# Attention and two MoE layers on one core: half of the mixed chunk's scores issued later, single scaling of maxima, and a higher rate of quad sums

## Chip, core and metric

The kernel runs on one core of one Trainium2 chip. The metric is the device time of one execution in microseconds (us). The engines are named as in the profile: PE (TensorE matmul) and PEld (its weight loads), DVE (VectorE), ACT (ScalarE), POOL (GpSimd), and SP (SyncE), which here only issues DMAs.

## What is computed

```python
# q, k, v: (4 batches, 12 heads, 448, 64); float32
q_n, k_n = rmsnorm(q, g_q), rmsnorm(k, g_k)
scores = q_n @ k_n.T / 8
scores = scores - max(scores, -1)
attn = exp(scores); attn = attn / sum(attn, -1)
x = (attn @ v)                         # to (1792, 768)
x = relu(x @ w_in) ** 2 @ w_out        # d_ff 2048
a, b = x @ w1, x @ w2                  # 768 -> 1024
out = ((a * b) @ w3) @ w_out2          # 1024 -> 1024 -> 768
```

## The kernel before

Every product is made from a high and a low part of each operand (three matmuls for one of float32), so PE has 5958 matmuls, most of 448 columns. The weights come in units of 128 rows; each is loaded by SP, split by ACT (high part) and by DVE or POOL (low part, line 150) into a tile named `hl`, and used by PE at lines 411 to 413.

A loop goes over 48 heads, `h` from 0 to 47, twelve to a batch; the text calls heads 0 to 11 batch one, 12 to 23 batch two and so on. Beside the attention of head `h`, `fill(n)` issues about `n` matmuls of the MoE of an earlier batch from a generator (`gen_moe`); what a call of `fill` issues beyond its number is taken off the next. So PE always has MoE matmuls between the attention's steps, and PE works in the order in which it is given its instructions.

The scores of a pair of heads (an even one and the odd one after it) are made in seven chunks of 128 queries: 0 to 3 for the even head, 4 to 6 for the odd one. Chunk 3 is mixed: 64 of its rows are the last queries of the even head, the other 64 belong to the odd head, so its first two matmuls read the odd head's transposed keys `kt`. These are made by `stage_k(h + 1)`: PE transposes (line 941), ACT copies the bank to SBUF (`kt<-kv`, line 144). From batch two on, `stage_k(h + 1)` stands one `fill` ahead of `stage_qk(h, 1)`, which makes chunks 2 and 3.

Each chunk's scores go to one of two PSUM banks (`ps_sc`). DVE takes the row maximum out of the bank (line 967, into a column of `nb`), ACT computes the exponentials from the bank (line 991, `p<-sc,nb,rr`), and only then may the bank be written again. In batch one (`h < H`) DVE also multiplies the maxima by `rq` (line 969), once for the two chunks of a stage; later ACT does that for each chunk (line 988). From batch two on the exponentials are written to SBUF as `p`, copied by a DMA to `pw` (line 1015), transposed by PE in four pieces `stage_t(h - 1, 0)` to `(h - 1, 3)` (line 1045) into two banks `pt`, and each of these is copied by ACT and has its low part subtracted by DVE (`ptr<-pt,ptr`, line 150, in `stage_lo`); then its bank is free.

For the last two batches the second MoE is computed by a scheme with sums of quarters ("quads") of its weights. `gen_sums` makes them: four loads (`quad<-f`, `quad<-w3o`), four subtractions on the engine that `drip` names, four stores (`qs<-quad`). `use`, called once for each weight unit that PE uses, calls `drip_one`, which lets `rate` such steps go. During the last `gen_moe` the engine is DVE. There, after each product `x @ w_in`, `relu2` has ACT take the relu `r` out of PSUM and square it, DVE make `gf` (line 487), and POOL make the low part of `act` (line 150) that PE needs in the product with `w_out`.

The order on each engine is set by a scheduler that goes by priorities and readiness; SP keeps the written order from batch three on, and all engines do in the last stretch.

Of the kernel before, what the change touches and what calls it, by code (L numbers as in the profile page):

```python
# [8 lines left out]
F32 = mybir.dt.float32  # L9
# [6 lines left out]
ALU = mybir.AluOpType  # L16
# [14 lines left out]
def attention_moe_kernel(  # L31
# [15 lines left out]
    nc = tc.nc  # L47
    SP, ACT, DVE, POOL, PE = (e.engine for e in (nc.sync, nc.scalar, nc.vector, nc.gpsimd, nc.tensor))
    B, P, H, C, D = k_nat.shape
# [6 lines left out]
    NFC = w_in.shape[0] // 2  # L56
    KX = w_in.shape[2] // 64
    NE = w_out.shape[0] // 4
# [36 lines left out]
    small = ctx.enter_context(tc.tile_pool(name="small", bufs=4))  # L95
# [170 lines left out]
    drip = {"eng": "g", "rate": 0.0, "due": 0.0}  # L266
# [294 lines left out]
    def later(steps, fn, *args):  # L561
        tasks.append((tail["now"] + steps, len(tasks), fn, args))
# [78 lines left out]
    def gen_pair():  # L641
# [36 lines left out]
        for e in range(NQ):  # L678
            later(2 + 4 * e, form3, 1, e)
            later(14 + 4 * e, form3, 2, e)  # L680
        drip.update(eng="v", rate=5 * 12 / (2 * NFC + 2 * NE))
        for y in gen_moe(B - 1, added):
            if tail["on"]:
                tick()
# [65 lines left out]
        n = NIC // 2  # L750
        todo4 = [(k, i) for k in ORDER4[1:] for i in range(n)]
        d = [{} for _ in range(NQ)]
# [38 lines left out]
    def load_group(g):  # L791
        if not (0 <= g < NH // GH):
            return
        b, h0 = divmod(g * GH, H)
        qk = t1.tile([128, GH * C, D], F32, name="qn", tag="qn")
        qn = qk[:, :GH // 2 * QC]
        kn = t2.tile([P, GH, C, D], F32, name="kn", tag="kn")
        if g == 0:
            nc.sync.dma_start(out=kn[:, 0:2], in_=k_nat[0, :, 0:2])
            load_head(0)  # L800
            nc.sync.dma_start(out=qn[:, :QC], in_=q_nat[0, :, 0])
            load_to(0)
            nc.sync.dma_start(out=kn[:, 2:], in_=k_nat[0, :, 2:GH])
            nc.sync.dma_start(out=qn[:, QC:], in_=q_nat[0, :, 1])
            load_to(1)
        else:
            nc.sync.dma_start(out=kn, in_=k_nat[b, :, h0:h0 + GH])
            nc.sync.dma_start(
                out=qn, in_=q_nat[b, :, h0 // 2:(h0 + GH) // 2].rearrange("p j c d -> p (j c) d")
            )  # L810
        grp[g] = [qk, kn, None, None]

    def load_head(h):
        if not (0 <= h < NH):
            return
        b, hh = divmod(h, H)
        t = t2.tile([128, S], F32, name="qt", tag="qt")
        nc.sync.dma_start(out=t, in_=q_t[b, hh])
        qts[h] = t

    def load_v(h):
        if not (0 <= h < NH):
            return
        b, hh = divmod(h, H)
        t = t2.tile([128, C, D], F32, name="v", tag="v")
        nc.sync.dma_start(out=t, in_=v_in[b, hh])
        vs[h] = t
# [115 lines left out]
        copy_on("a", kt, ps[:, :S].bitcast(F32))  # L943
        d["kt"] = kt

    def stage_qk(h, s):
        if not (0 <= h < NH):
            return
        d = heads[h]
        nb = d["nb"] = small.tile([128, 2], F32, name="nb", tag="nb")  # L950
        chunks = CHUNKS[h % 2][s]
        n = len(chunks)
        o = d["sc"] = [None] * n

        def score(out, d, at, m):
            nc.tensor.matmul(out, d["qh"][:, at:at + m], d["kt"], start=True, stop=False)  # L956
            nc.tensor.matmul(out, d["ql"][:, at:at + m], d["kt"], start=False, stop=True)  # L957

        for j, c in enumerate(chunks):
            ps = ps_sc.tile([128, 512], F32, name="sc", tag="sc")  # L960
            o[j] = ps[:, :S]
            if c == 3:
                score(o[j], heads[h + 1], S - 128, 128)
                score(o[j][:MIX], d, S - MIX, MIX)
            else:
                score(o[j], d, (c % 4) * 128, 128)
            nc.vector.tensor_reduce(out=nb[:, j:j + 1], in_=o[j], axis=AX.X, op=ALU.max, negate=True)  # L967
        if h < H:
            nc.vector.tensor_tensor(  # L969
                out=nb[:, :n], in0=nb[:, :n], in1=d["rq"][:, chunks[0]:chunks[0] + n], op=ALU.mult  # L970
            )

    def stage_exp(h, s):
        if not (0 <= h < NH):
# [143 lines left out]
    def fill(n):  # L1118
        state["credit"] += n
        while state["gen"] is not None and state["credit"] > 0:  # L1120
            try:
                k = next(state["gen"])
                state["credit"] -= k
                state["left"] -= k
            except StopIteration:
                state["gen"] = None
# [4 lines left out]
    def gen_late():  # L1131
# [15 lines left out]
        out=gg, in0=g_sb[:, 0:1], scalar=float(D) ** -0.5, in1=g_sb[:, 1:2], op0=ALU.mult, op1=ALU.mult  # L1147
# [8 lines left out]
    for h in range(NH + 1):  # L1156
        n = W3O / ((H + 1) * 6) if h <= H else (MOE / (H * 6) if h <= 2 * H else (MOE + IN) / (2 * H * 6))
        late = h > 2 * H
        if h < 2:
            load_head(h + 3)  # L1160
            load_v(h + 1)
        if not late and h % GH == 0:
            load_group(h // GH + 1)
        stage_qk(h, 0)
        fill(n)
        if h <= 2 * H + 1:
            stage_sums(h - 1)
        stage_exp(h, 0)
        if h > 2 * H:
            stage_words(h, 0)  # L1170
        if h == 0:
            group_prep(0, "rest")
        if h >= 2:
            load_head(h + 3)
            load_v(h + 1)
        if late and h % GH == GH - 1:
            load_group((h + 1) // GH + 1)
        if h % H != 1:
            stage_x(h - 2)
        stage_t(h - 1, 0)  # L1180
        stage_t(h - 1, 1)
        early = H <= h and h % 2 == 0
        fill(n)
        if early:
            stage_k(h + 1)
        stage_lo(h - 1)
        if h < NH:
            v_prep(h)
        fill(n)
        if h <= 2 * H:  # L1190
            stage_words(h, 0)
        stage_rows(h - 1)
        even = H <= h
        if even:
            stage_qk(h, 1)
        if not early:
            stage_k(h + 1)
        stage_t(h - 1, 2)
        stage_t(h - 1, 3)
        fill(n)  # L1200
        stage_lo(h - 1)
        if not even:
            stage_qk(h, 1)
            fill(n)
        stage_exp(h, 1)
        if h > 2 * H:
            stage_words(h, 1)
        fill(n)
        if even:
            fill(n)  # L1210
        if h <= 2 * H:
            stage_words(h, 1)
        stage_v(h - 1)
        if h >= 2 * H and h % GH < 2:
            group_prep(h // GH + 1, "qk"[h % GH])
        elif h % GH == 1:
            group_prep(h // GH + 1)
        head_prep(h + 2)
        if h and h % H == 0:
            if h != 3 * H:  # L1220
                fill(1e9)
            stage_x(h - 1)
            if h == H:
                start_fill(gen_moe(0), MOE)
            elif h == 2 * H:
                in_order(SP)
                start_fill(gen_late(), MOE + IN)
            elif h == NH:
                start_fill(gen_pair(), MOE)
# [61 lines left out]
```

## Time and profile before

| | |
|---|---|
| median of three runs | 1153.86 us (1152.88 to 1155.03) |
| the profiled execution's own time | 1159.42 us |
| its span, first to last instruction | 1157.6 us |
| mean granted clock of TensorE | 0.99 |
| busy: PE, DVE, ACT, POOL | 97%, 68%, 67%, 53% of the span |

The profiled execution took 0.48% longer than the median; durations and waits below are its own. Busy shares are means over stages of different kinds; PE's matmuls are pipelined, so that a busy PE can still be at half clock. The stretch of batch one is about 14 to 170 us, of batch two 170 to 416, of batches three and four 416 to 860; after that come the last MoE parts.

### The profile page before, as it was taken

The page shows a single profiled execution, that of the slowest core. Times are in us where ns is not written, and L with a number is a line of the kernel's source. Part 1 is how long each engine was busy: PE and PEld are TensorE (multiplying, and loading weights), DVE is VectorE, ACT ScalarE, POOL GpSimd, SP SyncE. Part 2 cuts the span into 40 slices and gives each one's busy share as a digit, 9 for nine tenths or more (in the row PEclk, how much of TensorE's full clock was granted, in tenths as well). Part 3 has the DMA queues.
Part 4 walks back from the last instruction along what each step waited for, and adds up shares of the span by engine and source line. Part 5 has one row for each costly group of instructions (what it writes and reads, how often), then busy time and mean ns, then how long its engine had stood idle before and what let it go on. Part 6 is the DMA issues. An engine that isn't in the chain of part 4 may idle for free.

```text
span 1157.6 us, 18785 instructions
## 1 busy us (share of the span) xinstructions
PE 1124.8 (97%) x5958; PEld 1019.5 (88%) x5958; DVE 790.3 (68%) x1363; ACT 776.6 (67%) x1768; POOL 608.9 (53%) x609
## 2 busy tenths in 40 slices
PE   7789999999999999999999999999999999999998
PEld 4678888999889899989989899999999899999997
DVE  6889888878898854565674755564544315887886
ACT  6889978888878866767776666776764435533352
POOL 3375433445545455957876776684865854011131
PEclk8899999999999999999999999999999999999999
DMA  7867757898998863565655657665556664243423
GB/s 237 264 201 211 235 160 243 306 297 293 321 294 276 279 190 120 165 213 178 219 172 163 207 182 236 197 197 165 171 170 202 215 193 126 69 135 105 130 83 123
DMA packets 130899, 229.74 MB, mean 198 GB/s; under 512 B 17472, under 2 KB 84544, under 8 KB 130800
## 3 DMA queue, kind: packets, MB, share of 16 engines
q1 hardware_dynamic: 129072, 225.79, 61.3%
q10 hardware_dynamic: 1728, 2.75, 0.7%
q8 instruction: 47, 0.77, 0.3%
q14 instruction: 52, 0.43, 0.1%
HBM read 162.53 MB, written 37.05 MB: 172 GB/s over the span
## 4 chain that ended last, share of the span: by engine, by line
PE 67%; ACT 12%; DMA 7%; DVE 7%; issue 3%; POOL 1%; SPq 1%; DVEq 0%; ACTq 0%; POOLq 0%
PE mm L411 16%; PE mm L412 16%; PE mm L413 16%; PE kv L1091 4%; PE pt L1045 3%; PE sc L956 2%; ACT p L991 2%; PE sc L957 2%; ACT raw L333 2%; ACT hl L144 2%; DMA raw<-wo 1%; DVE raw L346 1%; ACT ptr L144 1%; DMA raw<-w_in 1%; DMA raw<-w_out 1%
## 5 line engine op out<-in xcount | busy, mean ns | idle before, releaser
L150 POOL TENSOR_TENSOR hl<-raw,hl 128x384 fp32r<-128x384 f32 (+1 forms) x286 | 333.1, 1171 | 289.6 <-ACT hl L144 245.7
L144 ACT ACTIVATE hl<-raw 128x384 fp32r<-128x384 f32 (+1 forms) x405 | 227.8, 566 | 152.5 <-PE mm L413 40.1
L411 PE MATMUL mm<-x,hl 128*128 128x448 f32 (+1 forms) x640 | 238.3, 372 | 1.2 <-ACT x L144 1.2
L412 PE MATMUL mm<-x,hl 128*128 128x448 f32 (+1 forms) x640 | 234.2, 366 | 0.8 <-DVE x L150 0.8
L413 PE MATMUL mm<-x,hl 128*128 128x448 f32 (+1 forms) x640 | 233.7, 365 | 0.2 <-DVE hl L150 0.2
L411 PE MATMUL mm<-act,hl 128*128 128x448 f32 (+1 forms) x544 | 201.6, 371 | 1.9 <-ACT act L144 1.9
L412 PE MATMUL mm<-act,hl 128*128 128x448 f32 (+1 forms) x544 | 198.8, 365 | 3.7 <-DVE act L150 2.0
L413 PE MATMUL mm<-act,hl 128*128 128x448 f32 (+1 forms) x544 | 197.9, 364 | 0.1
L967 DVE TENSOR_REDUCE nb<-sc 128x1 f32<-128x448 f32 x168 | 102.6, 615 | 73.8 <-PE sc L957 72.4
L411 PEld LDWEIGHTS mm<-x,hl 128*128 128x128 f32 x640 | 121.0, 189 | 10.9 <-ACT x L144 2.3
L412 PEld LDWEIGHTS mm<-x,hl 128*128 128x128 f32 x640 | 121.0, 189 | 10.4 <-DVE x L150 1.8
L413 PEld LDWEIGHTS mm<-x,hl 128*128 128x128 f32 x640 | 120.9, 189 | 9.8 <-DVE hl L150 0.5
L991 ACT ACTIVATE p<-sc,nb,rr 128x448 f32<-128x448 f32 x168 | 121.3, 723 | 11.5 <-DVE nb L969 8.8
L150 DVE TENSOR_TENSOR ptr<-pt,ptr 128x512 fp32r<-128x512 f32 (+1 forms) x144 | 85.9, 617 | 57.9 <-ACT ptr L144 57.4
L412 PEld LDWEIGHTS mm<-act,hl 128*128 128x128 f32 x544 | 102.8, 189 | 12.3 <-DVE act L150 3.0
L411 PEld LDWEIGHTS mm<-act,hl 128*128 128x128 f32 x544 | 102.8, 189 | 9.5 <-ACT act L144 2.3
L413 PEld LDWEIGHTS mm<-act,hl 128*128 128x128 f32 x544 | 102.8, 189 | 8.0 <-DVE hl L150 0.4
L339 POOL TENSOR_SCALAR raw<-raw 128x384 uint32<-128x384 uint16 (+1 forms) x80 | 57.2, 716 | 83.1 <-DMA raw<-w_out 20.7
L346 DVE SCALAR_TENSOR_TENSOR raw<-raw 128x384 uint32<-128x384 uint32 (+1 forms) x120 | 86.4, 728 | 18.5 <-POOL raw L339 9.6
L956 PE MATMUL sc<-kt,qh 128*128 128x448 f32 (+1 forms) x192 | 74.8, 389 | 14.3 <-ACT p L991 7.4
L150 DVE TENSOR_TENSOR hl<-raw,hl 128x384 fp32r<-128x384 f32 (+1 forms) x119 | 80.0, 675 | 7.9 <-ACT hl L144 7.8
L333 ACT ACTIVATE raw<-raw 128x384 f32<-128x384 f32 (+1 forms) x120 | 71.6, 601 | 15.6 <-DMA raw<-w_in 7.7
(153 smaller groups left out, 2122.0 us busy)
## 6 DMA issues: line engine op xcount, KB each, us to landing
pw<-p SPq DMA_DIRECT2D x54, 448.0 KB
raw<-f_in SPq DMA_DIRECT2D x96, 192.0 KB
raw<-f_out SPq DMA_DIRECT2D x72, 256.0 KB
raw<-w_in SPq DMA_DIRECT2D x32, 384.0 KB
raw<-w_out SPq DMA_DIRECT2D x24, 512.0 KB
raw<-w SPq DMA_DIRECT2D x32, 384.0 KB
qt<-q_t SPq DMA_DIRECT2D x48, 224.0 KB
raw<-f SPq DMA_DIRECT2D x56, 192.0 KB
```

Of the source, the lines that this page charges most:

```text
L144: return nc.scalar.activation(out=out, in_=in_, func=AF.Copy)
L150: return (nc.vector if eng == "v" else nc.gpsimd).tensor_tensor(out=out, in0=in0, in1=in1, op=op)
L333: nc.scalar.activation(out=hi, in_=hi, func=AF.Prelu, scale=2.0**-112, alpha=-(2.0**32))
L339: nc.gpsimd.tensor_scalar(out=t[:, :n, 0], in0=low, scalar1=2.0**-13, scalar2=2.0**-14 - 0.5, op0=ALU.mult, op1=ALU.add)
L346: nc.vector.scalar_tensor_tensor(out=f[:, :n].bitcast(U32), in0=t[:, :n, 1], scalar=3, in1=t[:, :n, 0], op0=ALU.logical_shift_left, op1=AL ...
L411: nc.tensor.matmul(ps, w[:, 0, wk, :], x[0], start=(i == 0), stop=False)
L412: nc.tensor.matmul(ps, w[:, 0, wk, :], x[1], start=False, stop=False)
L413: nc.tensor.matmul(ps, w[:, 1, wk, :], x[0], start=False, stop=(i == last))
L956: nc.tensor.matmul(out, d["qh"][:, at:at + m], d["kt"], start=True, stop=False)
L967: nc.vector.tensor_reduce(out=nb[:, j:j + 1], in_=o[j], axis=AX.X, op=ALU.max, negate=True)
L991: nc.scalar.activation(out=p, in_=o[j], func=AF.Exp, scale=d["rq"][:, c:c + 1], bias=nb[:, j:j + 1], accum_out=sm[:, c:c + 1],)
L1091: nc.tensor.matmul(ps[:, :S], w, m, start=(n == 0), stop=(n == len(ops) - 1))
```

## The change

From batch two on, the stage's second chunk (the mixed one, of an even head) is no longer issued next to the first: the transposes `stage_t(h - 1, 2)` and `(h - 1, 3)` and half of the following `fill(n)` stand between them. In batch one each chunk's maximum is multiplied by itself, right behind its reduction, in place of one multiplication for the stage. The rate of the steps of the quad sums in the last `gen_moe` goes from 60/44 to 60/40 for each weight unit (`NFC` is 16, `NE` is 6).

```diff
-        drip.update(eng="v", rate=5 * 12 / (2 * NFC + 2 * NE))
+        drip.update(eng="v", rate=5 * 12 / (2 * NFC + 2 * NE - 4))
...
-    def stage_qk(h, s):
+    def stage_qk(h, s, part=None):
...
-        nb = d["nb"] = small.tile([128, 2], F32, name="nb", tag="nb")
         chunks = CHUNKS[h % 2][s]
-        n = len(chunks)
-        o = d["sc"] = [None] * n
+        if part != 1:
+            d["nb"] = small.tile([128, 2], F32, name="nb", tag="nb")
+            d["sc"] = [None] * len(chunks)
+        nb, o = d["nb"], d["sc"]
...
         for j, c in enumerate(chunks):
+            if part not in (None, j):
+                continue
...
             nc.vector.tensor_reduce(out=nb[:, j:j + 1], in_=o[j], axis=AX.X, op=ALU.max, negate=True)
-        if h < H:
-            nc.vector.tensor_tensor(
-                out=nb[:, :n], in0=nb[:, :n], in1=d["rq"][:, chunks[0]:chunks[0] + n], op=ALU.mult
-            )
+            if h < H:
+                nc.vector.tensor_tensor(
+                    out=nb[:, j:j + 1], in0=nb[:, j:j + 1], in1=d["rq"][:, c:c + 1], op=ALU.mult
+                )
...
         if even:
-            stage_qk(h, 1)
+            stage_qk(h, 1, 0)
         if not early:
             stage_k(h + 1)
         stage_t(h - 1, 2)
         stage_t(h - 1, 3)
-        fill(n)
+        if early:
+            fill(n / 2)
+            stage_qk(h, 1, 1)
+            fill(n / 2)
+        else:
+            fill(n)
```

Three places of the order show what this moves. The first is PE in head 18 (batch two): `sc` are score matmuls (the pair with 64 rows ends the mixed chunk), `pt` the transposes, `mm` the MoE. Before:

```order
L413 MATMUL mm<-x,hl 128x448
L956 MATMUL sc<-kt,qh 128x448
L957 MATMUL sc<-kt,ql 128x448
L956 MATMUL sc<-kt,qh 128x448
L957 MATMUL sc<-kt,ql 128x448
L956 MATMUL sc<-kt,qh 64x448
L957 MATMUL sc<-kt,ql 64x448
L1045 MATMUL pt<-ident_r,pw 128x128 x3
L1045 MATMUL pt<-ident_r,pw 64x128 x3
L411 MATMUL mm<-x,hl 128x448
```

The same place on PE in the changed kernel, whose lines have moved by one and by three:

```order
L413 MATMUL mm<-x,hl 128x448
L957 MATMUL sc<-kt,qh 128x448
L958 MATMUL sc<-kt,ql 128x448
L1048 MATMUL pt<-ident_r,pw 128x128 x3
L1048 MATMUL pt<-ident_r,pw 64x128 x3
L411 MATMUL mm<-x,hl 128x448
L412 MATMUL mm<-x,hl 128x448
L413 MATMUL mm<-x,hl 128x448
...
L957 MATMUL sc<-kt,qh 128x448
L958 MATMUL sc<-kt,ql 128x448
L957 MATMUL sc<-kt,qh 64x448
L958 MATMUL sc<-kt,ql 64x448
```

The mixed chunk's four matmuls now stand behind six transposes and six MoE matmuls (three of them left out above). So it is at the other even heads from 14 on, with nine MoE matmuls at 16 and 24; at head 12 the place is nearly as before.

The second place is DVE in batch one, at the second stage of head 6: two reductions of chunks 2 and 3 and the scaling of their maxima, `nb<-nb,rr`. Before:

```order
L967 TENSOR_REDUCE nb<-sc 128x1
L150 TENSOR_TENSOR ptr<-pt,ptr 128x384
L150 TENSOR_TENSOR pte<-pt,pte 64x384
L967 TENSOR_REDUCE nb<-sc 128x1
L863 TENSOR_REDUCE ss_107<-qn 112x16
L969 TENSOR_TENSOR nb<-nb,rr 128x2
L925 SCALAR_TENSOR_TENSOR ql<-qt,gg,qh 128x448
```

The same place on DVE in the changed kernel:

```order
L150 TENSOR_TENSOR pte<-pt,pte 64x384
L970 TENSOR_REDUCE nb<-sc 128x1 x2
L972 TENSOR_TENSOR nb<-nb,rr 128x1
L925 SCALAR_TENSOR_TENSOR ql<-qt,gg,qh 128x448
L972 TENSOR_TENSOR nb<-nb,rr 128x1
L346 SCALAR_TENSOR_TENSOR raw<-raw_1447 128x384
L863 TENSOR_REDUCE ss_107<-qn 128x14
```

The first maximum is scaled directly behind the two reductions, and a long reduction of another stage (line 863) no longer stands ahead of it. In all of batch one 42 such scalings stand where 24 stood, and many neighbours on every engine have changed places.

The third place is DVE in the last `gen_moe`, where PE makes `x @ w_in` for the first half (eight `gf`, here the first eight of the list), with the subtractions of three quads. Before:

```order
L487 TENSOR_TENSOR gf<-mm,r 128x448 x2
L150 TENSOR_TENSOR quad<-quad 128x512 x2
L487 TENSOR_TENSOR gf<-mm,r 128x448
L150 TENSOR_TENSOR quad<-quad 128x512 x2
L487 TENSOR_TENSOR gf<-mm,r 128x448 x3
L150 TENSOR_TENSOR quad<-quad 128x512
L487 TENSOR_TENSOR gf<-mm,r 128x448
L150 TENSOR_TENSOR quad<-quad 128x512 x3
L487 TENSOR_TENSOR gf<-mm,r 128x448
```

The same place on DVE in the changed kernel:

```order
L487 TENSOR_TENSOR gf<-mm,r 128x448 x2
L150 TENSOR_TENSOR quad<-quad 128x512 x4
L487 TENSOR_TENSOR gf<-mm,r 128x448 x4
L150 TENSOR_TENSOR quad<-quad 128x512 x3
L487 TENSOR_TENSOR gf<-mm,r 128x448
L150 TENSOR_TENSOR quad<-quad 128x512
L487 TENSOR_TENSOR gf<-mm,r 128x448
```

Ahead of the eighth `gf`, the last of the half, one subtraction stands where three stood, and three stand ahead of the seventh where one stood; on SP the loads of these quads stand up to one weight load earlier.

## Rows read from the trace of the kernel before

**Rows 1.** Page, parts 1 and 2: busy time; granted clock by fortieths of the span.

```profile
PE 1124.8 (97%) x5958; PEld 1019.5 (88%) x5958; DVE 790.3 (68%) x1363; ACT 776.6 (67%) x1768; POOL 608.9 (53%) x609
...
PEclk8899999999999999999999999999999999999999
```

**Rows 2.** PE's waits in the whole program: total us, times, longest.

```profile
PE sc L956 <- ACT p L991: 7.4, 8, 2.1
PE sc L956 <- ACT kt L144: 6.8, 7, 1.8
```

**Rows 3.** The same view from 165 to 420 us and from 420 to 870.

```profile
PE sc L956 <- ACT kt L144: 3.6, 3, 1.8
...
PE sc L956 <- ACT kt L144: 3.0, 3, 1.5
```

**Rows 4.** Timeline of PE, heads 18, 20, 22, 28, 32, 36: start, us, idle before.

```profile
292.79 0.36 PE L956 MATMUL sc<-kt,qh 128*128 128x448 f32 x1
292.99 0.37 PE L957 MATMUL sc<-kt,ql 128*128 128x448 f32 x1
294.87 0.47 PE L956 MATMUL sc<-kt,qh 128*128 128x448 f32 x1 [1.51 <-ACT kt L144]
...
295.79 0.38 PE L1045 MATMUL pt<-ident_r,pw 128*128 128x128 f32 x3
...
339.81 0.47 PE L956 MATMUL sc<-kt,qh 128*128 128x448 f32 x1 [0.35 <-ACT kt L144]
...
382.88 0.47 PE L956 MATMUL sc<-kt,qh 128*128 128x448 f32 x1 [1.75 <-ACT kt L144]
...
513.07 0.47 PE L956 MATMUL sc<-kt,qh 128*128 128x448 f32 x1 [1.48 <-ACT kt L144]
...
586.53 0.47 PE L956 MATMUL sc<-kt,qh 128*128 128x448 f32 x1 [0.92 <-ACT kt L144]
...
659.34 0.47 PE L956 MATMUL sc<-kt,qh 128*128 128x448 f32 x1 [0.58 <-ACT kt L144]
```

**Rows 5.** Timeline of DVE: low parts of the transposes, heads 18, 22, 28.

```profile
293.24 1.00 DVE L150 TENSOR_TENSOR ptr<-pt,ptr 128x384 fp32r<-128x384 f32 x2
...
380.36 1.02 DVE L150 TENSOR_TENSOR ptr<-pt,ptr 128x384 fp32r<-128x384 f32 x2 [0.37 <-ACT ptr L144]
...
511.28 1.02 DVE L150 TENSOR_TENSOR ptr<-pt,ptr 128x384 fp32r<-128x384 f32 x2 [2.09 <-ACT ptr L144]
```

**Rows 6.** Stretches behind two waits: busy us by engine, granted clock (PEclk), DMA.

```profile
384.40:387.70 3.30, 3.30 (x10) 2.91 (x10) 3.30 (x7) 2.63 (x7) 1.82 (x2) 0.50 0.85 299
...
513.10:516.50 3.40, 3.40 (x21) 3.04 (x22) 2.92 (x5) 3.22 (x10) 2.79 (x3) 1.00 0.85 225
```

**Rows 7.** Head 14: the mixed chunk's exponential on ACT, the next score in its bank.

```profile
216.16 0.76 ACT L991 ACTIVATE p<-sc,nb,rr 128x448 f32<-128x448 f32 x1
...
219.78 0.36 PE L956 MATMUL sc<-kt,qh 128*128 128x448 f32 x1
```

**Rows 8.** Batch one on DVE: a stretch, the scaling's group, its durations, one of them.

```profile
30.00:120.00 90.00, 78.77 (x412) 67.42 (x411) 82.73 (x150) 78.11 (x174) 49.77 (x56) 0.92 0.76 230
...
L969 DVE TENSOR_TENSOR nb<-nb,rr 128x2 f32<-128x2 f32 (+1 forms) x24 | 8.5, 354 | 0.1
...
L969 DVE TENSOR_TENSOR nb<-nb,rr x24: 143/158/1123, 18.8 to 169.5; 128x2 f32<-128x2 f32 x18, 128x1 f32<-128x1 f32 x6
...
114.42 1.01 DVE L969 TENSOR_TENSOR nb<-nb,rr 128x2 f32<-128x2 f32 x1
```

**Rows 9.** Timelines near 920 us: DVE, POOL, PE.

```profile
913.30 4.67 DVE L150 TENSOR_TENSOR quad<-quad 128x512 f32<-128x512 f32 x3 [0.59 <-DMA quad<-w3o]
917.89 0.61 DVE L487 TENSOR_TENSOR gf<-mm,r 128x448 f32<-128x448 f32 x1
...
918.65 1.13 POOL L150 TENSOR_TENSOR act<-gf,act 128x448 fp32r<-128x448 f32 x1 [1.23 <-DVE gf L487]
...
919.83 0.47 PE L412 MATMUL mm<-act,hl 128*128 128x448 f32 x1 [1.74 <-POOL act L150]
```

## Prediction

> **What bounds the kernel now.** I read the page first. PE is busy for 1124.8 of the span's 1157.6 us, and its granted clock falls short of full only in the first slices, which are batch one [rows 1]. So no engine beside PE can be worth much: what can be won is PE's idle time, about 33 us, and the time in which it runs at half clock. The next view is therefore PE's waits. Two kinds lead, both in front of score matmuls: 7.4 us in eight waits for an exponential (`ACT p`, the bank is not free) and 6.8 us in seven for the transposed keys (`ACT kt`) [rows 2]. By stretches, the waits for `kt` lie in batches two to four: 3.6 and 3.0 us [rows 3]. The timeline puts each of these in front of a mixed chunk, at heads 18, 20, 22, 28, 32 and 36, with 1.51, 0.35, 1.75, 1.48, 0.92 and 0.58 us, 6.6 in all [rows 4]. The waits for exponentials are nearly all in batch one. There DVE is as scarce as PE: from 30 to 120 us it is busy for 82.7 of 90 us, PE for 78.8 at a mean clock of 0.92 [rows 8]. One wait stands alone near the end, 1.74 us for the low part of an `act` [rows 9].
>
> **The mixed chunk.** The work is the same, only its place on PE differs: six transposes and six MoE matmuls go ahead of it. From a row's start to the next, a matmul takes 0.20 us at full clock (292.79 to 292.99) [rows 4], so six take 1.2 us and the chunk's own four 0.8; six transposes take about 0.4 (three run for 0.38 with their pipeline, the fourth starts some 0.2 behind the first). The keys thus get about 1.6 us more. Five of the six waits are shorter than that, the sixth (1.75) hardly longer.
>
> But the transposes now come earlier, and they have a wait of their own: the third piece needs the bank of the first, which is free when DVE has subtracted its low part. At head 18 these two subtractions run from 293.24 to 294.24, the first till about 293.75 [rows 5], while PE is done with chunk 2 at 292.99 + 0.20 = 293.2 [rows 4]. So piece three waits till 293.75 and piece four till 294.24, the latter is through at 294.45, the six matmuls at 295.65, the keys (there at 294.8) are not waited for, and the chunk's four end at 296.45. Before, the chunk began at 294.87, the transposes at 295.79, and the same work was through at 295.79 + 0.4 + 1.2 = 297.4. That is 0.95 won out of 1.51. At head 22 the subtractions end at 381.38 [rows 5], 0.2 too late for piece four alone, and the six matmuls reach 382.8, just when the keys come: some 0.05 us is left of the 1.75, so I count 1.7. At head 28 they end at 512.30, and by the same steps 512.3 + 0.2 + 1.2 + 0.8 = 514.5 against 513.07 + 0.92 + 1.6 = 515.6: 1.1. For 20, 32 and 36 I take the waits less 0.3 at head 32, where DVE is similarly late (estimate): 0.35 + 0.6 + 0.6. The sum is 0.95 + 1.7 + 1.1 + 1.55 = 5.3 us. Its upper bound is the 6.6 us of the waits.
>
> The wait of 1.75 us has a second price. From 384.4 to 387.7 us, 1.5 us behind it, PE is granted 0.50 of its clock, the 1.2 GHz level, and starts 10 matmuls; after the wait of 1.48 at 513.07 it keeps 1.00, the 2.4 GHz level, and starts 21 in 3.4 us [rows 6]. Half of that stretch is lost, 1.7 us, and I count it as won, since next to nothing is left of the gap. If the gap stays, so does this; bounds 0 and 1.7.
>
> What is late next: the mixed chunk's reduction, exponential and store come up to 1.6 us later where there was no wait to remove. The next user of its bank is chunk 5. At head 14, the tightest of the heads that move without having waited, the exponential ends at 216.92 and chunk 5 starts at 219.78: 2.9 us of slack [rows 7], more than 1.6. The store's issue on SP waits for that exponential and holds back the weight loads behind it by as much; since PE has no wait for a weight tile `hl` in these stretches (its waits there are nearly all those for `kt`) [rows 3], I cost that at nothing; without this cover it would cost up to 1.6 us once at each of the heads without a wait.
>
> **The single scaling in batch one.** 18 instructions are added on DVE. One takes 158 ns by the median, 354 by the mean, and 1123 at worst [rows 8]. By the median 18 cost 2.8 us, by the mean 6.4, and DVE has little idle time to hide them (7.3 of 90 us). Queued behind each is DVE's usual work: low parts of weights and of transposes, and the next reductions, for which ACT's exponentials wait.
>
> On the other side, an exponential of the first chunk no longer waits for the second reduction nor for what the scheduler has set between that and the scaling. The place shown in the change is such a case: a reduction of 1.1 us and the slow scaling at 114.42 (1.01 us) [rows 8] stood between. The waits that this can shorten are those 7.4 us [rows 2], and a wait that is taken from the first chunk's bank partly returns at the second's, since its maximum is not earlier. The order of batch one is reshuffled besides, on all engines, which no row prices. I set the net at 0, between a gain of 7.4 us (with a second clock drop of 1.7 avoided at best: 9.1) and a loss of 6.4, as the median cost of 2.8 is near the share of the waits that I would trust to go, four tenths.
>
> For why the mean is twice the median, the row shows single scalings of 1.0 to 1.1 us on tiles of 128x2 [rows 8]. The Trainium skill says in "SBUF — State Buffer", section "Who interferes with whom", that a VectorE instruction with two SBUF inputs, as this one is, contends with a GpSimd instruction that reads SBUF, and that this is an exclusive lock. By that rule each added scaling can stand behind a whole GpSimd subtraction, and the sum for batch one would be a loss of up to 18 × 1.0 us and not 0; the long durations in the trace agree with it, the median does not make it the usual case. What it would do here is the third rival.
>
> **The rate of the quad sums.** No work is added. At 913.30 three quad subtractions start, 4.67 us long, released by their loads; the eighth `gf` stands behind them, runs at 917.89, POOL makes the low part till 919.78, and PE waits 1.74 for it [rows 9]. Now one subtraction stands there (about 1.6 us, a third of 4.67), the other two ahead of the seventh `gf`, and their loads are issued up to one weight load earlier. With loads that come no earlier, two subtractions, `gf`, one subtraction would bring the eighth `gf` to about 913.3 + 3.1 + 0.6 + 1.6 = 918.6, 0.7 later than now. With loads earlier by one matmul group of a weight unit, 12 × 0.20 = 2.4 us, it is at 916.2, 1.7 earlier. I take the latter, 1.7 us, since the place in the order is earlier for the two loads that are waited for; bounds -0.7 and 1.74.
>
> **The sum.** 5.3 + 1.7 + 0 + 1.7 = 8.7 us, against the profiled execution's own 1159.42: 1150.7. That execution is longer than the median by 1159.42 / 1153.86 = 1.0048, so the forecast is 1150.7 / 1.0048 = **1145.2 us**, 0.75% faster.
>
> **Rivals.** (1) *The wait slides.* DVE, ACT and the loads set the pace of batch two, so that the keys of head 22 come no earlier when the wait at 18 is gone. For it: ACT and DVE stand close to PE in this stretch, and the subtractions above are late already. Against it: the wait falls behind a `fill` that ACT could use. Then batch two wins only the 1.6 us by which the chunk is moved, PE arrives early at head 22, the gap and the clock drop stay, and the sum is 1.6 + 1.1 + 1.2 + 1.7 = 5.6: 1148.3.
> (2) *Batch one wins.* The waits for exponentials go, and the clock drop behind the longest too: 9.1 more at most, half of it likelier: about 1140.7.
> (3) *The scaling loses the port.* Each added scaling costs as the one at 114.42, 1.01 us, all of it on the path, as DVE has no slack: 18.2 - 8.7 = 9.5 slower, 1163.3. It ends slower than before from (8.7 + 2.3) / 18 = 0.61 us each. For it: 92% busy DVE. Against it: the median of 158 ns. That it is GpSimd that holds them up is what the skill's page named above would say.
> (4) *It doesn't do what it says.* The transposes wait as long as the chunk did and the gain stays in the bank of the next reader, or the mean cost of the scaling (6.4) eats most of the rest: 1151.6 to 1153.
>
> **How the numbers follow.** Three runs of this kernel lie within 0.19%, so 0.2% (2.3 us) is about what a measurement can tell. I give the forecast (1143 to 1148.5 with its small bounds) 0.52, rival 1 0.14, rival 2 0.11, rival 4 0.13, rival 3 and any other loss of batch one's new order 0.10. Faster by over 0.2% are the forecast, rivals 1 and 2: 0.77; same 0.13; slower 0.10. The range leaves out the loss and the far end of rival 2 and reaches over rival 4: 1138.5 to 1154.
>
> **What would show it.** Right: no wait for `kt` over 0.3 us from batch two on, small waits of transposes for DVE instead at heads 18 and 28, the clock at 1.00 from batch two to the end, no wait for POOL near 918 us. The step on batch one is right if its scores still begin batch two at about 170 us. The prediction is wrong if batch one ends more than some 3 us earlier or later, if a new drop of the clock shows anywhere, or if the waits for `kt` return at other heads.

## The result and the profile after

The changed kernel takes 1157.74 us by the median of 18 runs (1155.39 to 1166.31), the kernel before 1153.34 in 18 runs beside them (1148.66 to 1159.02). The ratio, which is that of the mean times (1159.0 and 1153.1 us), is 1.0051, 95% interval 1.003 to 1.0072: **slower by 0.5%**, where 0.75% faster was forecast. (The medians alone give 1.0038.)

The profiled execution of the changed kernel took 1157.48 us, about its median. That of the kernel before, on which the forecast was built, took 1159.42, more than its kernel's median, so these two must not be set beside each other. I use a second profile of the kernel before, run as an experiment (own time 1152.58 us, median of its runs 1152.74).

PE's waits over the whole span of the changed kernel (what waited, for what, us in total, times, longest):

```profile
PE pt L1048 <- DVE ptr L150: 8.5, 13, 1.4
PE kv L941 <- DVE xf L1102: 3.7, 3, 2.3
...
PE pt L1048 <- DMA pw<-p: 2.2, 2, 1.6
PE sc L957 <- ACT p L994: 2.2, 2, 1.9
...
PE sc L957 <- ACT kt L144: 0.5, 2, 0.3
PE mm L412 <- POOL act L150: 0.5, 1, 0.5
```

The two waits that led before are nearly gone: 6.8 us for `kt` are 0.5, and 7.4 us for exponentials are 2.2 [rows 2]. Most of what the prediction named as the sign of success is there: no wait for `kt` is over 0.3 us, and the granted clock is 1.00 from 170 us to the end. Of the wait for POOL 0.5 us is left. In the place of the old waits the transposes `pt` wait for DVE's low parts and for the copy `pw`.

In batch one this is a plain exchange. From 0 to 170 us the second profile of the kernel before has

```profile
PE sc L956 <- ACT p L991: 6.8, 6, 2.1
...
PE pt L1045 <- DVE ptr L150: 0.4, 1, 0.4
```

and the changed kernel has

```profile
PE pt L1048 <- DVE ptr L150: 5.1, 7, 1.4
...
PE sc L957 <- ACT p L994: 2.2, 2, 1.9
```

PE waits less for ACT's exponentials and as much more for DVE's low parts; nothing is won. Two experiments below that have the scaling, e3 and h1, show the same there: 0.6 and 0.8 us for exponentials, 5.9 and 6.6 for low parts.

The stretch in which the time was lost shows in the starts of the first score of heads 12, 14 and 24. The timeline of PE in the second profile of the kernel before, and then in the changed kernel:

```profile
168.51 0.37 PE L956 MATMUL sc<-kt,qh 128*128 128x448 f32 x1
...
198.60 0.37 PE L956 MATMUL sc<-kt,qh 128*128 128x448 f32 x1
...
413.50 0.36 PE L956 MATMUL sc<-kt,qh 128*128 128x448 f32 x1
```

```profile
168.72 0.37 PE L957 MATMUL sc<-kt,qh 128*128 128x448 f32 x1
...
199.36 0.37 PE L957 MATMUL sc<-kt,qh 128*128 128x448 f32 x1
...
418.45 0.36 PE L957 MATMUL sc<-kt,qh 128*128 128x448 f32 x1
```

Batch one ends at the same time (168.5 and 168.7). From head 14 to head 24 the changed kernel takes 219.1 us against 214.9; behind that it takes 737.3 against 737.3 (spans 1155.7 and 1150.8). So by these two executions the loss lies in batch two, where nothing of the scaling was changed and where the chunk's waits were removed. (One kernel's two executions can differ by some 2 us in this stretch: the first profile of the kernel before has 216.7.)

### The profile page after: what moved, and what is told of

It reads as the page before. It is cut to its first block, busy times and chain, and to the rows that moved or that the text cites. A ratio compares the mean times of both kernels' runs of the same rounds, so it can differ in the third digit from the quotient of the medians.

```text
span 1155.7 us, 18789 instructions
## 1 busy us (share of the span) xinstructions
PE 1119.4 (97%) x5958; PEld 1015.1 (88%) x5958; DVE 801.2 (69%) x1381; ACT 778.3 (67%) x1768; POOL 605.3 (52%) x609
## 5 line engine op out<-in xcount | busy, mean ns | idle before, releaser
L346 DVE SCALAR_TENSOR_TENSOR raw<-raw 128x384 uint32<-128x384 uint32 (+1 forms) x120 | 92.9, 782 | 17.2 <-POOL raw L339 9.6
L150 DVE TENSOR_TENSOR hl<-raw,hl 128x384 fp32r<-128x384 f32 (+1 forms) x119 | 77.3, 653 | 7.4 <-ACT hl L144 7.3
L144 ACT ACTIVATE ptr<-pt 128x512 fp32r<-128x512 f32 (+1 forms) x144 | 74.7, 544 | 9.8 <-PE pt L1048 9.5
L333 ACT ACTIVATE raw<-raw 128x384 f32<-128x384 f32 (+1 forms) x120 | 70.9, 596 | 15.1 <-DMA raw<-w_out 4.2
```

Of the source, the lines that this page charges most:

```text
L144: return nc.scalar.activation(out=out, in_=in_, func=AF.Copy)
L150: return (nc.vector if eng == "v" else nc.gpsimd).tensor_tensor(out=out, in0=in0, in1=in1, op=op)
L333: nc.scalar.activation(out=hi, in_=hi, func=AF.Prelu, scale=2.0**-112, alpha=-(2.0**32))
L346: nc.vector.scalar_tensor_tensor(out=f[:, :n].bitcast(U32), in0=t[:, :n, 1], scalar=3, in1=t[:, :n, 0], op0=ALU.logical_shift_left, op1=AL ...
```

## The experiments

"Heads 14 to 24" is in each case the time between those two scores in the profile of that run; the ratio goes by the means of its runs and of those of the kernel before beside them (to within 0.0006), with its 95% interval.

| run | what it has | ratio | heads 14 to 24, us |
|---|---|---|---|
| e1_before_again | the kernel before | 0.9999 (0.9977 to 1.002) | 214.9 |
| e2_chunk_only | later mixed chunk | 0.9985 (0.9963 to 1.0006) | 212.2 |
| e3_scaling_only | single scaling | 1.0067 (1.0044 to 1.0091) | 220.3 |
| e4_rate_only | new rate | 1.000 (0.998 to 1.002) | 213.1 |
| f1_scaling_old_order | e3, order of before from head 12 | 1.0061 (1.0046 to 1.0076) | 214.7 |
| f2_only_new_order | before, order of e3 from head 12 | 1.0063 (1.0038 to 1.0088) | 219.8 |
| f3_only_scalings | before and 18 scalings, all else in its place | 1.0017 (0.9995 to 1.0038) | 212.3 |
| f4_after_old_order | all edits, order without scaling from head 12 | 1.003 (1.0014 to 1.0046) | 212.7 |
| h1_scaling_old_from14 | e3, order of before from head 14 | 1.0033 (1.0015 to 1.0052) | 215.1 |
| h2_only_new_from14 | before, order of e3 from head 14 | 1.0032 (1.001 to 1.0053) | 219.7 |
| h3_after_old_from14 | all edits, order without scaling from head 14 | 1.013 (1.01 to 1.0161) | 218.9 |
| h4_chunk_and_rate | later chunk, new rate | 0.997 (0.995 to 0.999) | 212.9 |
| i1_one_place_new | before, one place as in h2 | 1.0015 (0.9996 to 1.0033) | 218.0 |
| i2_one_place_old | h2, that place as before | 1.0015 (0.9995 to 1.0034) | 216.4 |
| i3_all_edits_good_order | all edits, order of h4 throughout | 0.9983 (0.9963 to 1.0003) | 212.4 |
| i4_chunk_and_rate_again | h4 again | 0.9972 (0.9947 to 0.9996) | 211.1 |

### The parts by themselves

Three theories stood at the start: the loss is the single scaling's, by its instructions and by the new order of batch one; it is the moved chunk's, in batch two; or the rate adds to it at the end.

**e1**, the kernel before, unchanged.

> The kernel before, unchanged, for a second profile of it. If the profiled execution of before was an unlucky one, its early stretch will differ: batch two's first score then starts 3 us or more away from 169.9 us, and the clock stands at half in other stretches than before. If the 6.6 us of waits for the transposed keys belong to the program and not to that execution, they show again at heads 18, 22 and 28, within 0.5 us each. Ratio to the kernel before: 1.000.

**e2**, the later chunk (with the parameter `part` of `stage_qk`, as in the change):

```diff
...
         if even:
-            stage_qk(h, 1)
+            stage_qk(h, 1, 0)
...
-        fill(n)
+        if early:
+            fill(n / 2)
+            stage_qk(h, 1, 1)
+            fill(n / 2)
+        else:
+            fill(n)
```

> The later mixed chunk alone, with the old scaling and the old rate; batch one is then ordered as before. Theory 1 (the loss is the 18 scalings and the new order of batch one; the later chunk wins a little): 2 to 5 us faster, ratio 0.996 to 0.998. Theory 2 (the later chunk brings the transposes to PE before DVE has freed their banks and the stores before the next head needs them, so batch two loses): slower by 2 to 5 us, ratio 1.002 to 1.004, with batch two some 3 us longer than before and batches three and four some 3 us shorter.

**e3**, the single scaling:

```diff
-        if h < H:
-            nc.vector.tensor_tensor(
-                out=nb[:, :n], in0=nb[:, :n], in1=d["rq"][:, chunks[0]:chunks[0] + n], op=ALU.mult
-            )
+            if h < H:
+                nc.vector.tensor_tensor(
+                    out=nb[:, j:j + 1], in0=nb[:, j:j + 1], in1=d["rq"][:, c:c + 1], op=ALU.mult
+                )
```

> The single scaling of maxima in batch one alone. Theory 1: it carries the loss, 4 to 7 us slower, ratio 1.0035 to 1.006, and batch one ends later by as much. Theory 2: within 1.5 us of before, ratio 0.999 to 1.001.

**e4**, the rate:

```diff
-        drip.update(eng="v", rate=5 * 12 / (2 * NFC + 2 * NE))
+        drip.update(eng="v", rate=5 * 12 / (2 * NFC + 2 * NE - 4))
```

> The higher rate of the quad sums alone; every engine has the old order up to the last MoE. Both theories: 1 to 2 us faster, ratio 0.998 to 0.999, the wait for POOL near 918 us falls from 1.7 to under 0.5 us. A third theory, that the quads' subtractions ahead of the seventh product cost as much as they save ahead of the eighth: ratio 1.000 with a new wait of 1 us or more nearby.

The scaling alone loses 0.67%, the chunk wins about 0.15% (its interval holds zero), the rate does nothing that can be measured. So the scaling carries the loss. But e3's profile shows the same puzzle as that of the changed kernel: its batch one ends at 170.1 us, close to the 166.5 to 169.9 of e1, e4 and the first profile, and its heads 14 to 24 are the longest of the table. Something that the scaling caused acts from some 30 to 250 us after the last scaling has run.

### The order, taken apart from the edit

What the scaling changes in batch two is the order that the scheduler chose there for ACT, DVE, POOL and SP. PE's order from head 14 on is the same, and so are the instructions. To test this, an order can be held fixed: a table says, for each engine, where each instruction stood in the order of another kernel, and dependencies without a semaphore tie each instruction to the one ahead of it, so that the scheduler has no choice left.

```diff
-    chain()
+    chain(), pin(nc, tc)
...
+def pin(nc, tc):
...
+        for p, i in zip(row, row[1:]):
+            tc.add_manual_dep(i, p.name, why, reason="pinned order")
```

Theory A: the order of batch two costs the time. Theory B: the scalings do, by DVE's time in batch one and what they leave undone for later. f1 and f2 exchange the order from head 12 on, f3 adds the 18 scalings and leaves every other instruction in its place, and f4 gives the changed kernel the order that it has without the scaling.

> The single scaling alone, as in the run before that cost 0.67%, but from head 12 on all five engines are held to the order that the kernel before has there; batch one up to about 130 us keeps the order that came with the scaling. Theory A (the loss comes from the other order that the scheduler then chose in batch two, not from the 18 scalings): ratio 0.998 to 1.002 to the kernel before, batch two (first score of head 12 to that of head 24) 243 to 247 us. Theory B (the scalings themselves, by DVE's time in batch one and by what they leave undone for batch two): 1.004 to 1.009 again, batch two 249 us or more, with waits for kt of over 2 us at heads 16 and 18.

> The kernel before with its scaling of two columns; from head 12 on all five engines are held to the order that the kernel with the single scaling has there. Nothing is added or moved but by this order. Theory A: slower by 0.4% to 0.9%, batch two 249 to 253 us, a wait for kt of some 2.5 us near 255 us. Theory B: no change (0.998 to 1.002), batch two 243 to 247 us.

> The 18 scalings are added and nothing else: each stands on DVE right behind its reduction (in the first stage of head 0 next to the other), and all other instructions of all engines stand in the order of the kernel before, from the first to the last. This is the price of the instructions themselves. Theory A: 0 to 2 us (0.998 to 1.002), since batch one ended at the same time with and without them. Theory B: 5 to 9 us slower (1.004 to 1.008).

> The changed kernel with all three of its edits, but from head 12 on in the order that the later chunk and the new rate give without the single scaling. Theory A: the loss of 0.5% is gone, 0.996 to 1.001, batch two 242 to 245 us. Theory B: as the changed kernel, 1.003 to 1.007, batch two 248 us or more.

f2 and f3 speak for A: the order alone, with no instruction added, loses 0.63%, and the scalings alone, with no order changed, 0.17% (the interval holds zero), whatever the holding of the order costs included. But f1 lost as well, which A had not expected, and f4 kept 0.3%. Their profiles show where: from head 14 on both are short again (214.7 and 212.7 us), but from the first score of head 8 to that of head 14 f1 takes 80.5 us (123.7 to 204.2), against 76.1 in h1 (123.5 to 199.6), whose batch one is left as the scheduler made it. In f1 the granted clock is 0.50 there from 144.9 to 148.3 us and from 179.0 to 182.4 us. f2 also has 78.1 us there, against 75.1 in e1, so its 0.63% is not the order of batch two alone. Instructions of batch one and two lie side by side there, and I take it that fixing the one kind pushed the other out of place: a cost of the seam between the two orders, argued and not tested. The next set puts the seam at head 14 and keeps the places of both kinds.

> The single scaling alone with its own order through batch one and heads 12 and 13, untouched this time; from head 14 on each engine has, at the same places of its order, the sequence of the kernel before. PE's order is not changed by this at all. Theory A (the order from head 14 to head 24 costs 5 to 7 us): first score of head 14 to that of head 24 in 212 to 216 us in place of 220, ratio 0.999 to 1.003. Theory B (what batch one leaves undone is missing later, whatever the order): 218 to 221 us in that stretch and a ratio of 1.005 to 1.008.

> The kernel before, untouched through head 13; from head 14 on ACT, DVE, POOL and SP have the sequence of the kernel with the single scaling, at the same places; PE's order is that of the kernel before from first to last. No instruction is added. Theory A: 219 to 221 us from head 14 to head 24, ratio 1.004 to 1.007. Theory B: 212 to 216 us, ratio 0.998 to 1.002.

> The changed kernel with all its edits, untouched through head 13; from head 14 on each engine has the sequence that the later chunk and the new rate give without the single scaling, PE as it was. Theory A: 211 to 214 us from head 14 to head 24 in place of 219, ratio 0.997 to 1.001. Theory B: 217 us or more, ratio 1.003 to 1.007.

> The changed kernel without the single scaling, in its own order: the later chunk and the new rate. Both theories: 0.996 to 1.000, as the later chunk alone gave 0.9985 and the rate alone 1.000.

h1 and h2 came out in the middle: each has half of e3's loss. Before and e3 are the other two corners of a square, and its sides add up: 0.33% for the scaling with its order up to head 13, 0.32% for the order from head 14 on, 0.67% for both, each within some 0.2%. In heads 14 to 24 the old order has 212.3 to 216.7 us in six profiles of the unmoved chunk (the first profile, e1, e4, f1, f3, h1), the new order 219.7 to 220.3 in three (e3, f2, h2). All three of these, and two of the six (the first profile and h1), hold one stretch of 3.4 us at half clock, worth 1.7 us; without it the ranges are 212.3 to 215.0 and 218.0 to 218.6. So A holds for that stretch, but explains about half of e3's loss. h3 missed both theories: it lost more than either allows, at the seam. PE waits there 5.9 us for an `x` in front of head 14, whose first score comes at 208.2 in place of 199.4, and heads 14 to 16 take 48.1 us in place of 43.4. The two orders that I joined do not fit at head 14. Behind head 16 it is as quick as h4: 170.8 and 170.9 us to head 24 (256.3 to 427.1, 239.3 to 410.1), 175.7 in the changed kernel (242.7 to 418.4).

### One place of the order, and all edits in one good order

Which place does it? The first long wait in the new order is at head 16. Here ACT in h2, start, duration, line, and in brackets the idle time before and what ended it:

```profile
232.28 0.58 ACT L144 ACTIVATE acc<-mm 128x448 f32<-128x448 f32 x1
232.70 0.67 ACT L144 ACTIVATE hl<-raw 128x512 fp32r<-128x512 f32 x1
233.95 0.55 ACT L333 ACTIVATE raw<-raw 128x384 f32<-128x384 f32 x1 [0.57 <-DMA raw<-w_in]
234.40 0.53 ACT L144 ACTIVATE kt<-kv 128x448 fp32r<-128x448 f32 x1
234.82 0.60 ACT L144 ACTIVATE ptr<-pt 128x512 fp32r<-128x512 f32 x1
...
249.69 0.56 ACT L333 ACTIVATE raw<-raw 128x384 f32<-128x384 f32 x1 [1.89 <-DMA raw<-w_in]
...
253.96 0.54 ACT L333 ACTIVATE raw<-raw 128x384 f32<-128x384 f32 x1 [1.15 <-DMA raw<-w_in]
254.41 0.54 ACT L337 ACTIVATE raw<-raw 128x384 uint32<-128x384 uint16 x1
254.85 0.52 ACT L144 ACTIVATE osb<-mm 128x448 f32<-128x448 f32 x1
255.27 0.53 ACT L144 ACTIVATE kt<-kv 128x448 fp32r<-128x448 f32 x1
```

And DVE in h2 at the first of these places:

```profile
233.45 0.62 DVE L967 TENSOR_REDUCE nb<-sc 128x1 f32<-128x448 f32 x1
235.40 0.56 DVE L346 SCALAR_TENSOR_TENSOR raw<-raw 128x384 uint32<-128x384 uint32 x1 [1.33 <-POOL raw L339]
235.87 0.82 DVE L925 SCALAR_TENSOR_TENSOR ql<-qt,gg,qh 128x448 fp32r<-128x448 f32 x1
236.61 0.68 DVE L150 TENSOR_TENSOR ptr<-pt,ptr 128x512 fp32r<-128x512 f32 x1
```

A step of a weight load (L333 on ACT, L346 on DVE) stands ahead of the attention's copies and low parts. Its load has only just landed, so ACT stands still 0.57 us, and DVE 1.33 for POOL's part of the same step, and what is queued behind them is late. Fifteen us on, ACT stands still for loads 1.89 and 1.15 us with a copy of `kt` behind them. PE in h2 at that copy:

```profile
255.85 0.50 PE L956 MATMUL sc<-kt,qh 128*128 128x448 f32 x1 [2.19 <-ACT kt L144]
```

And h2's window behind it (sum; PE, PEld, DVE, ACT and POOL busy; clock, DMA share, GB/s):

```profile
256.00:259.50 3.50, 3.50 (x14) 2.90 (x15) 0.97 (x2) 1.18 (x3) 1.32 (x3) 0.52 0.99 324
```

A wait of 2.19 us, and then a granted clock of 0.52, close to the 1.2 GHz level, for the window. i1 puts only this place of the new order into the kernel before, i2 puts it back in h2. i3 has all three edits in one order that fits throughout, that of h4.

> The kernel before with one place of its order changed, near 230 to 246 us: on ACT, DVE and POOL the steps of a weight load (the first w_in of a new group) stand ahead of the copy of kt and of the low parts of the transposes, as in the order that came with the single scaling (12 + 2 rows of ACT, 6 + 3 of DVE, 4 of POOL). If this place carries the loss: a wait for kt of about 2 us at head 16 (near 255 us), perhaps with a drop of the clock of 1.7 us behind it, heads 14 to 18 in 86 to 88 us in place of 83 to 84, ratio 1.002 to 1.004. If the loss is spread over many places: heads 14 to 18 in 83 to 85 us, ratio 0.998 to 1.002.

> The run with the new order from head 14 on (ratio 1.0032), with this one place put back into the order of the kernel before. If the place carries the loss: no wait for kt over 0.5 us near 255 us, heads 14 to 18 in 83 to 85 us, ratio 0.999 to 1.002. If not: 86 to 88 us, ratio 1.002 to 1.005.

> The changed kernel, all three edits, in the order that the later chunk and the new rate have without the single scaling, on all engines from the first instruction to the last; the 18 scalings stand behind their reductions. If only the order is at fault: 0.996 to 1.000. If the scalings themselves cost what the run with them alone left possible (0.17%): 0.9985 to 1.001. If the loss is the scalings', 1.003 or more.

> The later chunk and the new rate without the single scaling, a second time: 0.995 to 0.999, as in the first (0.997).

ACT in i2, the same place:

```profile
230.07 0.64 ACT L144 ACTIVATE hl<-raw 128x512 fp32r<-128x512 f32 x1
230.59 0.54 ACT L144 ACTIVATE kt<-kv 128x448 fp32r<-128x448 f32 x1
231.02 0.60 ACT L144 ACTIVATE ptr<-pt 128x512 fp32r<-128x512 f32 x1
...
233.10 0.57 ACT L333 ACTIVATE raw<-raw 128x384 f32<-128x384 f32 x1
...
248.15 0.56 ACT L333 ACTIVATE raw<-raw 128x384 f32<-128x384 f32 x1 [0.34 <-DMA raw<-w_in]
...
249.47 0.54 ACT L144 ACTIVATE kt<-kv 128x448 fp32r<-128x448 f32 x1
```

Here `kt` and the copies go first, and the later stop for a load ahead of the next `kt` is 0.34 us (one of 2.02 us, at 252.85, comes behind that copy). The wait at head 16 follows the place. In i2 it is under 0.2 us (2.19 in h2), and heads 14 to 18 take 83.5 us against 87.6. In i1 it is there with 0.94 us, none of this size stands there in e1, and heads 14 to 18 take 84.6 against 83.9. The loss as a whole cannot be put down to it: i1 and i2 both come out at 1.0015, which for i1 is what a loss spread over many places was expected to give and for i2 what a loss of this place was; both intervals reach both cases. And i2's next two waits for `kt` are 2.42 and 1.47 us. The place decides one wait; the rest must lie at other places, which I have not taken apart.

i3 settles the main question. It runs the same instructions as the changed kernel, 18 single scalings among them, and its ratio is 0.9983 in place of 1.0051. Its timeline at heads 14 and 24:

```profile
199.13 0.37 PE L957 MATMUL sc<-kt,qh 128*128 128x448 f32 x1
...
411.50 0.36 PE L957 MATMUL sc<-kt,qh 128*128 128x448 f32 x1
```

PE's waits in i3 from 286 to 420 us:

```profile
PE pt L1048 <- DVE ptr L150: 1.0, 3, 0.4
PE kv L941 <- DVE xf L1102: 0.5, 1, 0.5
```

The same window of the changed kernel:

```profile
PE pt L1048 <- DMA pw<-p: 2.2, 2, 1.6
PE pt L1048 <- DVE ptr L150: 2.0, 3, 1.0
PE kv L941 <- DVE xf L1102: 1.1, 1, 1.1
```

Heads 14 to 24 take 212.4 us in place of 219.1, and before and behind this stretch the two agree (199.1 and 199.4 to head 14; 737.0 and 737.3 from head 24 to the end). In five profiles of the moved chunk without the new order (e2, f4, h4, i3, i4) the stretch takes 211.1 to 212.9 us. Of the 6.7 us, 3.8 are in these waits. How long PE is busy in the stretch, in the changed kernel and in i3:

```profile
199.36:418.45 219.09, 213.08 (x1139) 1.00 0.88 288
```

```profile
199.13:411.50 212.37, 210.83 (x1139) 1.00 0.90 294
```

That is 6.0 us idle against 1.5, at full clock in both: 4.5 of the 6.7 us are idle time of PE, nearly all in front of transposes.

The fastest version is h4 and i4, the changed kernel without the single scaling: 0.997 and 0.9972, 0.3% faster than before. i3 against these two gives 0.12% for the scalings, f3 against the kernel before 0.17%: 1.4 to 2 us, with intervals that hold zero.

## Why the prediction was wrong, step by step

**What bounds the kernel: right.** PE's waits for `kt` and for exponentials were there again in the second profile (5.7 and 6.8 us), and removing those for `kt` is worth something: 0.3% together with the rate (h4, i4). That removing those for exponentials is worth anything no run shows; in the changed kernel they came back as waits for DVE (above). One reading of the page was too short: a 9 in its clock row stands for 0.9 and more, so the row does not show the 3.4 us at half clock near 385 us, which the prediction itself uses.

**The mixed chunk: right in kind, too large.** In the second profile of the kernel before, PE's waits from 170 to 830 us are these:

```profile
PE sc L956 <- ACT kt L144: 5.5, 5, 1.5
PE pt L1045 <- DVE ptr L150: 0.8, 1, 0.8
PE pt L1045 <- DMA pw<-p: 0.2, 1, 0.2
```

In h4, the later chunk with the rate, they are these:

```profile
PE pt L1049 <- DVE ptr L150: 2.4, 4, 0.8
PE kv L941 <- DVE xf L1103: 1.2, 2, 0.8
```

So 6.5 us became 3.6, in i4 2.1 and in e2 3.6: 2.9 to 4.4 us won, where the term was 5.3. What stayed, most of it the transposes' waits for DVE, is more than the 1.3 us that the step left over, and in h4 it lies at heads 18, 22, 36 and 38, where the step had named 18 and 28. By time, e2 won 0.15%, with an interval that holds zero.

**The clock drop of 1.7 us: not there to be won each time.** It belonged to the execution that was read. In e1 the wait at head 22 is 0.95 us and no drop follows. It follows a wait of 2.08 us in h1, 2.20 in i1, 2.19 in h2 (above) and 2.60 at 258.6 in e3, but not one of 2.56 at 302.0 in e3 or of 2.42 at 293.0 in i2.

**The rate: too large, nothing that could be measured.** The term was 1.7, the wait for POOL near 918 us in one execution [rows 9]. It is 0.76 us in the second profile of the same kernel, 1.52 in f3 and 0.50 in f2, none of which has the edit; with the edit it is 0.47 in e4 and in the changed kernel. Over all profiles it is 0.28 to 1.74 us in the eleven without the edit, 0.96 by the mean, and 0.47 to 0.50 in the seven with it. So the edit does shorten this wait, by half a us on the mean and 1.3 at most, and e4's ratio is 1.000 (0.998 to 1.002), too coarse to show that.

**The single scaling: the step that failed.** The prediction set its net at 0 and said that the order of batch one is reshuffled besides, "on all engines, which no row prices". The instructions themselves were sized well: the group on DVE in the changed kernel (minimum, median, maximum in ns) is

```profile
L972 DVE TENSOR_TENSOR nb<-nb,rr x42: 108/153/1249, 17.1 to 167.1; 128x1 f32<-128x1 f32 x42
```

and f3 prices all 18 at some 2 us (0.17%, at most 0.38% by its interval), far from rival 3's 18.2, so rival 3 was wrong too. The long ones exist, but they are few. Eleven of the 42 took over 200 ns; each of these began while a POOL instruction ran, and ten of them ended 1 to 21 ns behind the end of that one, the eleventh 91. The longest, in the changed kernel:

```profile
57.72 1.25 DVE L972 TENSOR_TENSOR nb<-nb,rr 128x1 f32<-128x1 f32 x1
```

```profile
57.21 1.74 POOL L150 TENSOR_TENSOR hl<-raw,hl 128x512 fp32r<-128x512 f32 x1
```

POOL ends at 58.95 us, DVE at 58.97. The Trainium skill says in "SBUF — State Buffer", section "Who interferes with whom", that a VectorE instruction with two SBUF inputs contends with a GpSimd instruction that reads SBUF; the eleven agree with it.

Batch one ended on time, which the prediction had named as the test of this step. What it left out is that the reshuffle does not end with batch one. The order of DVE, ACT, POOL and SP differs up to about 420 us, and this costs 0.32% from head 14 on in the kernel before (h2), plus a smaller part ahead of it (h1 less f3, 0.16%, not resolved). In the changed kernel the new order costs 0.68% (1.0051 against i3's 0.9983), some 7.8 us. The prediction read the new order at the places where an edit stood, and held the rest to be the same work as before.

In the sum: 8.7 us faster was forecast. Without the scaling 3.3 us faster was measured (0.29%, h4 and i4), and with it 5.9 us slower (0.51%). So chunk, clock and rate were set 5.4 us too high, and the scaling, set at 0, cost 9.2 us, of which its own instructions are about 1.4 (i3 against h4 and i4, an interval that holds zero). The prediction gave a loss by the new order a chance of 0.10, of batch one's order only, and left it out of the range. None of its signs of being wrong appeared in the changed kernel, since they look at the waits that the edits touch, at the clock and at the end of batch one.

The forecast of 1145.2 us would have been 0.5% too low even with the good order (i3: 1151.2), by the chunk, the clock and the rate; its sign would probably have been right (0.9983, interval up to 1.0003).

**What stays open:** which places beside the one of i1 and i2 make up the rest of the order's loss, and how the loss ahead of head 14 divides between scalings and order.

## What to carry to other kernels

Where a scheduler sets the order, an edit of a few tiny instructions can cost more by the order that it brings about a few hundred us later than by itself: compare the orders to the end, and look for steps that wait on a load and now stand ahead of work that PE waits for. To learn what an edit is worth, hold the order fixed and run both halves apart (same edit, other order; other order, no edit), and join two orders only where they meet cleanly: two of my seams, at head 12 and in h3, cost several us of their own. A single wait in one profiled execution is no term of a sum until a second execution shows it with the same size.

## What the runs showed of the hardware

I had not expected PE's matmuls to have two rhythms at the same clock. From 940 to 1140 us PE never waits; the window (PE busy, matmuls started, clock, DMA) of the changed kernel is

```profile
940.00:1140.00 200.00, 200.00 (x988) 1.00 0.36 112
```

and that of h1 is

```profile
940.00:1140.00 200.00, 200.00 (x969) 1.00 0.38 114
```

That is 202.4 against 206.4 ns for each, with the granted clock at 1.00 in both. Five of the 18 profiles (e3, e4, h1, h3, i2) are of the slower kind. In each of them it begins behind one of PE's last waits, between 910 and 926 us, and lasts to the end. In h1 a start follows the other after 202.7 ns by the mean up to the wait at 910, and after 206.7 behind it. From head 46's first score to the end these five take 329.8 to 332.6 us, the others 325.6 to 327.1, so it costs some 3 us or more. It may be part of the scatter between runs of one kernel; no kernel here has a profile of each kind, so that isn't shown. What decides between the two I don't know.
